# Batch 0 of a fused attention and MLP kernel: four neighbouring tokens per partition, x loaded head by head, scores by pairs of heads

## The chip, the cores and the metric

The kernel runs on one core of one Trainium2 chip. The metric is the device time of a launch in microseconds (us); a profiled execution of the same program gives the spans, busy times and waits. Engines in the profile: PE is TensorE (PEld its weight loads), DVE is VectorE, ACT is ScalarE, POOL is GpSimd, SP is SyncE; ACTq and SPq are the queues from which ScalarE and SyncE issue DMAs. A line number such as L197 is a line of the kernel before.

## The reference

A block-recurrent cross attention between tokens x and a small state, followed by an MLP with the activation `h * erf(softplus(h))` over all tokens and states. All shapes are fixed:

```python
B, H, S, Ns, D = (8, 8, 512, 32, 64)          # x: (B,H,S,D), state: (B,H,Ns,D), float32
scores  = softmax(scale * x @ state^T)        # tokens read the state
xread   = scores @ state
scores2 = softmax(scale * state @ x^T)        # the state reads the tokens
sread   = scores2 @ x
x = concat([xread, sread], axis=2)  ->  (B * (S + Ns), H * D) = (4352, 512)
h   = x @ w_in                                # (512, 2048)
g   = h * erf(softplus(h))
out = g @ w_out                               # (2048, 512)
```

Tokens of a batch are independent in everything but the sum over tokens in `sread`. So they may be kept in any order inside the kernel, as long as the rows of `out` are written back in theirs.

## The kernel before

One core works through the eight batches one after the other. A batch's tokens need x with the features on the partitions (`xT`: for pair i of heads, 64 features of head 2i on partitions 0 to 63 and 64 of head 2i+1 on partitions 64 to 127). For batches 1 to 7 this is made far ahead. Batch 0 is the start of the program, and nothing can run before it, so it has its own code, `attention0`. Meanwhile the weights, which come as float64 and are converted to float32 on ScalarE and VectorE, are loaded behind x on the SyncE queue.

Loads of batch 0. x is loaded in four quarters of 128 tokens, token 128c+p on partition p; one head's part of a token is 64 floats, 256 bytes:

```python
x_t[0] = xin.tile([P, NC, H, D], F32, name="x")
for c in range(NC):                                            # L108
    (nc.scalar, nc.sync)[c % 2].dma_start(
        out=x_t[0][:, c], in_=x[0, :, P * c:P * c + P].rearrange("h p d -> p h d"))
for e in range(2):
    nc.sync.dma_start(out=st[:, 0, D * e:D * e + D],
                      in_=state[0].rearrange("(i e) n d -> e i n d", e=2)[e])
# ... and then, on the same queue, the weights
```

Filler products keep TensorE working while it would wait:

```python
def warm(n):
    for _ in range(n):
        last = nc.tensor.matmul(out=spare[:, 0:P], lhsT=ident, rhs=ident, start=True, stop=True)
```

The score products (state against tokens, contraction over 64 features). There are eight, two (e = 0, 1) for each pair of heads i, and each fills its own 64x32 part of the array:

```python
def scored(b, xT):
    s2 = [ps_at.tile([P, S], F32, name="at") for _ in range(2)]
    for i in reversed(range(NI)):
        for e in range(2):
            r, q = slice(D * e, D * e + D), slice(Ns * i, Ns * i + Ns)
            on_pe = nc.tensor.matmul(out=s2[e][q, :], lhsT=st[r, b, q], rhs=xT[r, i, :],
                                     start=True, stop=True)     # L197
    ...
```

The opening of batch 0. TensorE transposes 128 tokens of two heads at a time; the four quarters are taken as they land. Then four copies, two on ScalarE and two on VectorE, bring the four pairs from PSUM to `xT`; the state is turned; then the scores:

```python
warm(8)                                                         # in the main program, before
...
def attention0(between):
    xt = x_t[0]
    xT = att.tile([P, NI, S], F32, name="xT")
    xp = [ps_o.tile([P, S], F32, name="o%d" % i) for i in range(3)]
    xp.append(ps_h.tile([P, S], F32, name="h"))
    for c in 1, 0, 2, 3:
        if c == 2:
            warm(3)
        for i in range(NI):
            nc.tensor.transpose(out=xp[i][:, P * c:P * c + P],  # L304
                                in_=xt[:, c, 2 * i:2 * i + 2, :], identity=ident)
    for i in range(NI):
        (nc.scalar.copy, nc.vector.tensor_copy)[i % 2](xT[:, i, :], xp[i])   # L307
    states(range(1), ps_h, "h")                                 # L182, L183
    s2 = scored(0, xT)                                          # L197
    between[0]()            # 32 fillers; the first weight conversion on ScalarE
    ...
    a = states_weights(0, s2, both)   # VectorE: 32x32 transposes (L217), max, subtract; ScalarE: exp
    ...                               # sums, normalise, transposes (L321): aT, with weights converted between
```

After that come the first projection (L714), the activation and the second projection (L550) of batch 0's first column group. The order of the instructions on TensorE, VectorE, ScalarE and SyncE is held fixed in this part as written.

The output rows of a batch are stored by quarters, 2 KB to a row:

```python
def put_x(b, h):
    rows = out[TB * b:TB * b + S].rearrange("(c p) e -> c p e", p=P)
    def go(r, ot, c=slice(0, d_model)):
        nc.sync.dma_start(out=rows[2 * h + r][:, c], in_=ot[:, c])
```

Of the kernel before, what the change touches and what calls it, by code (L numbers as in the profile page):

```python
# [8 lines left out]
F32 = mybir.dt.float32  # L9
# [7 lines left out]
def kernel(  # L17
# [17 lines left out]
    nc = tc.nc  # L35
    B, H, S, D = x.shape
    Ns = state.shape[2]
    d_model, d_ff = moe_w_in.shape
    P = 128
    NI = H // 2  # L40
    NC = S // P
# [4 lines left out]
    TB = S + Ns  # L46
# [5 lines left out]
    xin = ctx.enter_context(tc.tile_pool(name="xin", bufs=1))  # L52
# [6 lines left out]
    ps_at = ctx.enter_context(tc.tile_pool(name="ps_at", bufs=2, space=PSUM))  # L59
# [3 lines left out]
    ident = const.tile([P, P], F32, name="ident")  # L63
    make_identity(nc, ident)

    x_t = {}


    def load_x(b):
        t = xin.tile([P, NC, H, D], F32, name="x")  # L70
        for h in range(H):
            nc.sync.dma_start(out=t[:, :, h, :], in_=x[b, h].rearrange("(c p) d -> p c d", p=P))
        x_t[b] = t
# [30 lines left out]


    st = const.tile([P, B, P], F32, name="st")
    x_t[0] = xin.tile([P, NC, H, D], F32, name="x")
    for c in range(NC):  # L108
        (nc.scalar, nc.sync)[c % 2].dma_start(
            out=x_t[0][:, c], in_=x[0, :, P * c:P * c + P].rearrange("h p d -> p h d"))  # L110
    for e in range(2):
        nc.sync.dma_start(out=st[:, 0, D * e:D * e + D],
                          in_=state[0].rearrange("(i e) n d -> e i n d", e=2)[e])

    def load_st():
        for h in range(H):
            i, e = h // 2, h % 2
            nc.sync.dma_start(out=st[Ns * i:Ns * i + Ns, 1:B, D * e:D * e + D],
                              in_=state[1:B, h].rearrange("b n d -> n b d"))
# [46 lines left out]
    def warm(n):  # L166

        for _ in range(n):
            last = nc.tensor.matmul(out=spare[:, 0:P], lhsT=ident, rhs=ident, start=True,
                                    stop=True)  # L170
        return last
# [5 lines left out]
    def states(bs, pool=ps_at, name="at"):  # L177


        ps = pool.tile([P, len(bs), P], F32, name=name)  # L180
        for k, b in enumerate(bs):
            last = nc.tensor.transpose(out=ps[:, k], in_=st[:, b, :], identity=ident)  # L182
        nc.scalar.copy(st[:, bs[0]:bs[-1] + 1, :], ps)  # L183
        return last
# [2 lines left out]

    marks = []

    def scored(b, xT):  # L190


        s2 = [ps_at.tile([P, S], F32, name="at") for _ in range(2)]
        for i in reversed(range(NI)):
            for e in range(2):
                r, q = slice(D * e, D * e + D), slice(Ns * i, Ns * i + Ns)
                on_pe = nc.tensor.matmul(out=s2[e][q, :], lhsT=st[r, b, q], rhs=xT[r, i, :],  # L197
                                         start=True, stop=True)
        marks.append(on_pe)
        return s2  # L200
# [10 lines left out]
    def states_weights(b, sc, both):  # L211

        aT[b] = keep.tile([P, 2, S], F32, name="aT")
        a = both[:, 0:2].rearrange("p e (k n) -> p e k n", n=Ns)
        m1 = small.tile([P, 2, NC * NI], F32, name="m1")
        for e in range(2):
            nc.vector.transpose(out=both[:, e], in_=sc[e])  # L217
        for e in range(2):
            nc.vector.reduce_max(out=m1[:, e], in_=a[:, e], axis=AX.X)
        for e in range(2):  # L220
            nc.vector.tensor_tensor(a[:, e], a[:, e], over(m1[:, e]), op=ALU.subtract)
            nc.scalar.activation(out=a[:, e], in_=a[:, e], func=ACTF.Exp, scale=scale)
        return a

    def sums(a):
        z1 = small.tile([P, 2, NC * NI], F32, name="z1")
        for e in range(2):
            nc.vector.reduce_sum(out=z1[:, e], in_=a[:, e], axis=AX.X)
        return z1

    def normalise(a, z1):
        nc.vector.tensor_scalar(z1, z1, 1e-9, None, op0=ALU.add)
        nc.vector.reciprocal(z1, z1)
        for e in range(2):
            nc.vector.tensor_tensor(a[:, e], a[:, e], over(z1[:, e]), op=ALU.mult)

    def largest(sc):
        m2 = small.tile([P, 2], F32, name="m2")
        for e in range(2):
            nc.vector.reduce_max(out=m2[:, e:e + 1], in_=sc[:, e], axis=AX.X)  # L240
        nc.vector.tensor_scalar(m2, m2, -scale, None, op0=ALU.mult)
        return m2

    def weigh_tokens(sc, m2, a2):

        z2 = small.tile([P, 2], F32, name="z2")
        for e in range(2):
            nc.scalar.activation(out=a2[:, e], in_=sc[:, e], func=ACTF.Exp, bias=m2[:, e:e + 1],
                                 scale=scale, accum_out=z2[:, e:e + 1])
        return z2  # L250

    def inverse(z):
        nc.vector.tensor_scalar(z, z, 1e-9, None, op0=ALU.add)
        nc.vector.reciprocal(z, z)

    def turn_weights(a2):
        a2T = att.tile([P, 2, NC, P], F32, name="sc")
        for e in range(2):
            ps = ps_at.tile([P, NC, P], F32, name="at")
            for c in range(NC):  # L260
                nc.tensor.transpose(out=ps[:, c, :], in_=a2[:, e, P * c:P * c + P],
                                    identity=ident)
            nc.scalar.copy(a2T[:, e], ps)
        return a2T
# [3 lines left out]
    def read_tokens(b, a2T, z2, pool=ps_at, name="at"):  # L268


        xt = x_t.pop(b)
        sr = pool.tile([P, 2, D], F32, name=name)
# [3 lines that stand above are left out]
                    q = slice(Ns * i, Ns * i + Ns)  # L276
                    nc.tensor.matmul(out=sr[q, e, :], lhsT=a2T[:, e, c, q],  # L277
                                     rhs=xt[:, c, 2 * i + e, :],
                                     start=(c == 0), stop=(c == NC - 1))
        sn = sn_t[b] = const.tile([P, 2, D], F32, name="sn0") if b == 0 else \  # L280
            st[:, b - 1, :].rearrange("p (e d) -> p e d", e=2)
        for e in range(2):
            nc.vector.tensor_scalar(sn[:, e], sr[:, e], z2[:, e:e + 1], None, op0=ALU.mult)
# [8 lines left out]
    def attention0(between):  # L292

        xt = x_t[0]
        xT = att.tile([P, NI, S], F32, name="xT")
        xp = [ps_o.tile([P, S], F32, name="o%d" % i) for i in range(3)]
        xp.append(ps_h.tile([P, S], F32, name="h"))
        for c in 1, 0, 2, 3:  # L300
            if c == 2:
                warm(3)
            for i in range(NI):
                nc.tensor.transpose(out=xp[i][:, P * c:P * c + P],  # L304
                                    in_=xt[:, c, 2 * i:2 * i + 2, :], identity=ident)
        for i in range(NI):
            (nc.scalar.copy, nc.vector.tensor_copy)[i % 2](xT[:, i, :], xp[i])  # L307
        states(range(1), ps_h, "h")
        s2 = scored(0, xT)
        between[0]()  # L310
        both = att.tile([P, NI, S], F32, name="xT")
        sc = att.tile([P, 2, S], F32, name="sc")
        a = states_weights(0, s2, both)
        for e in range(2):
            nc.scalar.copy(sc[:, e], s2[e])
        between[1]()
        z1 = sums(a)
        between[2]()
        normalise(a, z1)
        for e in range(2):  # L320
            nc.vector.transpose(out=aT[0][:, e], in_=both[:, e])  # L321

        def rest():
            a2 = both[:, 2:4]
            m2 = largest(sc)
            yield
            z2 = weigh_tokens(sc, m2, a2)
            inverse(z2)
            yield
            a2T = turn_weights(a2)  # L330
            yield
            read_tokens(0, a2T, z2)
            yield

        return rest()
# [9 lines left out]
    def attention(b, xT=None):  # L345
# [40 lines left out]
        if b + 1 < B:  # L386
            load_x(b + 1)
# [231 lines left out]
        put(0, o1, slice(E2, d_model))  # L619

    def put_x(b, h):
        rows = out[TB * b:TB * b + S].rearrange("(c p) e -> c p e", p=P)

        def go(r, ot, c=slice(0, d_model)):
            nc.sync.dma_start(out=rows[2 * h + r][:, c], in_=ot[:, c])
        return go
# [118 lines left out]
    def amid_sums():  # L745
# [4 lines left out]
        warm(5)  # L750

    rest = attention0((after_scores, before_sums, amid_sums))
    g0 = group()

# [113 lines left out]
    xT, _ = turn_x(1)  # L868
# [7 lines left out]
    turn = attention(1, xT)  # L876
# [40 lines left out]
    at = [combine_a(1)]  # L917
# [8 lines left out]
    def pending():  # L926
        yield from seconds
        store(acc, lambda r, ot: put_x(0, r // 2)(r % 2, ot))

    for b in range(1, B + 1):  # L930
# [4 lines left out]
        for g, (first, second) in enumerate(groups):  # L935
# [5 lines left out]
            if b + 1 < B:  # L941

                late = b == 1
                if g == late:
                    side[6 if late else 6] = (lambda: behind(marks, next, turn)) if late else \
                        lambda old=turn: (next(old), behind(marks, next, turn))
                    turn = attention(b + 1)
# [64 lines left out]
```

## Time and profile before

Three runs gave a median of 732.15 us (732.14 to 732.15). The profiled execution spans 730.7 us.

| what | before |
|---|---|
| TensorE busy | 721.6 us, 99% of the span |
| VectorE, ScalarE busy | 524.0 us (72%), 395.6 us (54%) |
| first TensorE instruction | 1.35 us |
| first transpose of x on TensorE | 4.92 us |
| third quarter of x starts its transposes | 7.95 us |
| score products start | 10.30 us |
| VectorE's first transpose of the scores | 11.57 us |
| first projection, first product (L714) | 22.10 us |
| second projection, first product (L550) | 31.01 us |
| x of batch 0, issue to landing | 4.1 to 6.7 us for each 256 KB |

How to read it: in a timeline a row is a run of like instructions of one engine, with its start, the time from the first start to the last end, the number of records and, in square brackets, the idle time of the engine just before it and what ended it. A TensorE instruction can leave more than one record. Ends of TensorE records are modelled, so that start-to-start distances say more than durations. In the table of windows each row is a stretch of the span, with the busy time of each engine in it.

### The profile page before, as it was taken

The numbers are of one execution on the slowest core, as the hardware profiler recorded it, in microseconds if no ns is written. First come the engines' busy times: TensorE is split into PE (matmuls) and PEld (weight loads), VectorE is DVE, ScalarE is ACT, GpSimd is POOL, SyncE is SP. The second block draws the span as 40 slices with busy tenths as digits, with TensorE's granted clock in tenths as the row PEclk, the third lists the DMA queues.
The fourth block names the chain that finished last, engine by engine and source line by source line (L and its number), as shares of the span: only waits on it lengthen the run. The fifth ranks groups of instructions, "written<-read, shape, count | busy, mean of one in ns | idle before, by whom it ended". The sixth has DMA issues, their size and how long they took to land.

```text
span 730.7 us, 12128 instructions
## 1 busy us (share of the span) xinstructions
PE 721.6 (99%) x5016; PEld 588.0 (80%) x5016; DVE 524.0 (72%) x766; ACT 395.6 (54%) x498; POOL 0.7 (0%) x6
## 2 busy tenths in 40 slices
PE   8899999999999999999999999999999999999998
PEld 7434435889889888988989888988898899999996
DVE  4988887997798677867587669866686756674423
ACT  4898894665556444754455445544575434443340
POOL 0000000000000000000000000000000000000000
PEclk9999999999999999999999999999999999999999
DMA  7577842330153203310061104220111000000001
GB/s 234 174 216 241 224 94 58 87 59 30 19 99 67 50 1 66 80 30 30 1 144 27 33 1 94 60 44 9 38 50 30 30 1 30 1 30 1 30 1 29
DMA packets 139166, 46.40 MB, mean 64 GB/s; under 512 B 126696, under 2 KB 130536, under 8 KB 139112
## 3 DMA queue, kind: packets, MB, share of 16 engines
q1 hardware_dynamic: 136840, 44.92, 24.6%
q10 hardware_dynamic: 2272, 0.72, 0.5%
q8 instruction: 39, 0.64, 0.4%
q14 instruction: 15, 0.12, 0.1%
HBM read 33.03 MB, written 8.91 MB: 57 GB/s over the span
## 4 chain that ended last, share of the span: by engine, by line
PE 92%; DVE 2%; ACT 1%; issue 0%; ACTq 0%
PE o L600 50%; PE h L493 27%; PE o L550 7%; PE at L407 2%; PE h L407 1%; PE h L714 1%; PE at L197 1%; PE at L421 1%; PE h L277 1%; DVE s L727 0%; PE at L277 0%; DVE hs L721 0%; ACT L724 0%; DVE w_out L148 0%; ACT s L724 0%
## 5 line engine op out<-in xcount | busy, mean ns | idle before, releaser
L600 PE MATMUL o<-w_out,s 128*128 128x256 f32 x480 | 118.0, 380 | 0.0
L600 PE MATMUL o<-raw,hs 128*128 128x256 f32 x480 | 117.3, 382 | 0.0
L500 ACT ACTIVATE s<-hs 128x512 f32<-128x512 f32 x120 | 75.4, 630 | 74.3 <-DVE hs L501 74.0
L600 PE MATMUL o<-w_out,hs 128*128 128x256 f32 x480 | 114.1, 380 | 0.0
L600 PEld LDWEIGHTS o<-raw,hs 128*128 128x128 f32 x480 | 89.9, 190 | 22.6 <-issue 10.9
L501 DVE TENSOR_TENSOR hs<-hs,h 128x512 f32<-128x512 f32 x90 | 61.8, 687 | 62.6 <-PE h L493 62.4
L600 PEld LDWEIGHTS o<-w_out,hs 128*128 128x128 f32 x480 | 90.8, 190 | 16.3 <-issue 4.2
L600 PEld LDWEIGHTS o<-w_out,s 128*128 128x128 f32 x480 | 84.6, 191 | 7.9
L501 DVE TENSOR_TENSOR hs<-s,h 128x512 f32<-128x512 f32 x60 | 41.1, 685 | 67.6 <-PE h L493 67.1
L493 PEld LDWEIGHTS h<-aT,m 128*128 128x128 f32 x672 | 83.8, 192 | 4.3 <-issue 1.4
L493 PE MATMUL h<-aT,m 128*128 128x128 f32 x672 | 84.4, 275 | 0.0
L545 DVE TENSOR_TENSOR s<-s,hs 128x2048 f32<-128x2048 f32 (+1 forms) x31 | 68.8, 2218 | 20.4 <-ACT s L543 20.4
L504 ACT COPY s<-h 128x512 f32<-128x512 f32 x29 | 17.0, 585 | 107.7 <-PE h L493 107.7
L550 PE MATMUL o<-w_out,s 128*128 128x512 f32 x128 | 59.1, 600 | 0.6 <-DVE s L727 0.5
L493 PE MATMUL h<-sy,sx 128*128 128x128 f32 x448 | 59.4, 275 | 0.0
L493 PEld LDWEIGHTS h<-sy,sx 128*128 128x128 f32 x448 | 56.7, 192 | 2.1 <-issue 0.5
L543 ACT ACTIVATE s<-s 128x2048 f32<-128x2048 f32 x30 | 57.4, 1912 | 0.3
L509 ACT COPY hs<-h 128x512 f32<-128x512 f32 x29 | 17.0, 585 | 74.8 <-PE h L493 74.8
L600 PE MATMUL o<-raw,s 128*128 128x256 f32 x240 | 56.8, 379 | 0.0
L550 PEld LDWEIGHTS o<-w_out,s 128*128 128x128 f32 x128 | 23.1, 190 | 31.1 <-issue 25.8
L600 PEld LDWEIGHTS o<-raw,s 128*128 128x128 f32 x240 | 43.5, 190 | 4.7
L500 ACT ACT_TABLE_LOAD x31 | 39.8, 1283 | 0.5
(133 smaller groups left out, 915.4 us busy)
## 6 DMA issues: line engine op xcount, KB each, us to landing
raw<-in_moe_w_in_dram SPq DMA_DIRECT2D x8, 1024.0 KB, 5.7
raw<-in_moe_w_out_dram SPq DMA_DIRECT2D x8, 1024.0 KB, 4.8
xq<-in_x_dram SPq DMA_DIRECT2D x112, 64.0 KB, 2.2
x<-in_x_dram SPq DMA_DIRECT2D x56, 128.0 KB, 2.8
out_dram<-ot SPq DMA_DIRECT2D x18, 256.0 KB, 2.2
sc<-xT SPq DMA_DIRECT2D x112, 32.0 KB, 1.9
out_dram<-ot SPq DMA_DIRECT2D x28, 128.0 KB, 1.9
x<-in_x_dram ACTq DMA_DIRECT2D x2, 256.0 KB, 5.7
```

The source lines that it names most:

```text
L197: on_pe = nc.tensor.matmul(out=s2[e][q, :], lhsT=st[r, b, q], rhs=xT[r, i, :], start=True, stop=True)
L277: nc.tensor.matmul(out=sr[q, e, :], lhsT=a2T[:, e, c, q], rhs=xt[:, c, 2 * i + e, :], start=(c == 0), stop=(c == NC - 1))
L407: nc.tensor.matmul(out=ps[k][e][q, :], lhsT=st[r, b, q], rhs=w_in[r, 2 * g:2 * g + 2, i, :], start=True, stop=True)
L493: last = nc.tensor.matmul(out=bank[:, q], lhsT=lhsT, rhs=rhs, start=(first and i == 0 and k == 0), stop=(i == GF - 1 and k == len(ops) - 1 ...
L500: nc.scalar.activation(out=s[:, k], in_=hs[:, k], func=ACTF.Softplus)
L501: add = lambda o, x, y: nc.vector.tensor_tensor(o, x, y, op=ALU.add)
L504: copy(m1, p)
L509: copy(c11, p)
L543: nc.scalar.activation(out=s, in_=s, func=ACTF.Erf)
L545: nc.vector.tensor_tensor(s[:, k], s[:, k], hs[:, k], op=ALU.mult)
L550: nc.tensor.matmul(out=acc[r], lhsT=gT[:, i, P * r:P * r + P], rhs=w_out[:, GF * g + i, :], start=(g == 0 and i == 0), stop=(g == NG - 1 a ...
L600: nc.tensor.matmul(out=acc[bank][:, E2 * c:E2 * c + E2], lhsT=lhs[:, i, :], rhs=rhs[:, g, i, :], start=(first and i == 0 and c == 0), stop ...
```

## The change

Four things change, all for batch 0:

- Partition p holds the tokens 4p to 4p+3, so that one head's part of a partition is 1 KB in a row, in DRAM and on the chip.
- x is loaded head by head, the even heads on ScalarE's queue and the odd heads on SyncE's, with the state's two halves after the first head of each.
- TensorE turns x one pair of heads at a time. With heads outside and tokens inside, a pair's features no longer lie side by side, so each head is turned by itself, by a plain product with the identity into its half of the partitions. The copies to `xT` and the score products follow pair by pair, behind the turning of the next pair.
- The rows of `out` of batch 0 are stored in the new order (row 4p+c instead of 128c+p).

It is meant to bring x in larger runs and to start on the first heads while the last ones are still under way.

```diff
-    x_t[0] = xin.tile([P, NC, H, D], F32, name="x")
-    for c in range(NC):
-        (nc.scalar, nc.sync)[c % 2].dma_start(
-            out=x_t[0][:, c], in_=x[0, :, P * c:P * c + P].rearrange("h p d -> p h d"))
-    for e in range(2):
-        nc.sync.dma_start(out=st[:, 0, D * e:D * e + D],
-                          in_=state[0].rearrange("(i e) n d -> e i n d", e=2)[e])
-
+    x_t[0] = xin.tile([P, H, NC, D], F32, name="x").rearrange("p h c d -> p c h d")
+
+    def load_x0(queue, h, n):
+        queue.dma_start(out=x_t[0][:, :, h:h + n, :].rearrange("p c h d -> p h c d"),
+                        in_=x[0, h:h + n].rearrange("h (p c) d -> p h c d", c=NC))
+
+    def load_st0(queue, e):
+        queue.dma_start(out=st[:, 0, D * e:D * e + D],
+                        in_=state[0].rearrange("(i e) n d -> e i n d", e=2)[e])
+
+    for i in range(NI):
+        for e, queue in enumerate((nc.scalar, nc.sync)):
+            load_x0(queue, 2 * i + e, 1)
+            if i == 0:
+                load_st0(queue, e)
@@
-    def scored(b, xT):
-        s2 = [ps_at.tile([P, S], F32, name="at") for _ in range(2)]
-        for i in reversed(range(NI)):
+    def scored(b, xT, s2=None, pairs=tuple(reversed(range(NI)))):
+        s2 = s2 or [ps_at.tile([P, S], F32, name="at") for _ in range(2)]
+        for i in pairs:
@@
-        for c in 1, 0, 2, 3:
-            if c == 2:
-                warm(3)
-            for i in range(NI):
-                nc.tensor.transpose(out=xp[i][:, P * c:P * c + P],
-                                    in_=xt[:, c, 2 * i:2 * i + 2, :], identity=ident)
-        for i in range(NI):
+        s2 = [ps_at.tile([P, S], F32, name="at") for _ in range(2)]
+
+        def turn(i):
+            for c in range(NC):
+                for e in range(2):
+                    nc.tensor.matmul(out=xp[i][D * e:D * e + D, P * c:P * c + P],
+                                     lhsT=xt[:, c, 2 * i + e, :], rhs=ident, start=True,
+                                     stop=True)
             (nc.scalar.copy, nc.vector.tensor_copy)[i % 2](xT[:, i, :], xp[i])
+
+        turn(0)
         states(range(1), ps_h, "h")
-        s2 = scored(0, xT)
+        turn(1)
+        warm(2)
+        scored(0, xT, s2, (0,))
+        turn(2)
+        scored(0, xT, s2, (1,))
+        turn(3)
+        scored(0, xT, s2, (2,))
+        warm(3)
+        scored(0, xT, s2, (3,))
@@
-        rows = out[TB * b:TB * b + S].rearrange("(c p) e -> c p e", p=P)
+        rows = out[TB * b:TB * b + S].rearrange("(p c) e -> c p e" if b == 0 else
+                                                "(c p) e -> c p e", p=P)
```

(The new `scored` loop body is the old one.)

## The prediction

> **What bounds the kernel now.** I read three views: the table of windows by stage over the whole run (how much can a change at the start be worth, and is it given back later?), the timeline of the first 22 us (which instruction ends last before the first projection work), and the list of waits of the opening (which of those ends are waits for data).
>
> ```profile
> core 0: us, PE busy (x) PEld busy (x) DVE busy (x) ACT busy (x) POOL busy (x), PEclk, DMA share, GB/s
> 0.00:5.00 5.00, 3.65 (x17) 3.60 (x18) 0.00 (x0) 1.28 (x1) 0.70 (x6) 1.00 0.66 135
> 5.00:11.57 6.57, 5.29 (x42) 3.90 (x42) 1.29 (x2) 1.32 (x4) 0.00 (x0) 1.00 1.15 327
> 11.57:22.10 10.53, 9.26 (x90) 8.52 (x90) 10.33 (x17) 8.90 (x12) 0.00 (x0) 1.00 0.48 172
> 22.10:31.00 8.90, 8.01 (x32) 3.02 (x32) 8.74 (x11) 7.00 (x10) 0.00 (x0) 1.00 0.56 197
> 31.00:60.00 29.00, 28.70 (x94) 11.90 (x95) 24.67 (x27) 27.12 (x31) 0.00 (x0) 1.00 0.75 233
> ```
>
> From 31 us on TensorE is the bound (28.70 of 29.00 us busy, then 69.63 of 70 and 570.00 of 570 in the later rows of the same answer). Between 11.57 and 31 us VectorE is (10.33 of 10.53 and 8.74 of 8.90 us). Only the first 11.57 us, up to the end of batch 0's scores, have no such full engine, and the change lies wholly in them. What follows is in fixed order on each engine, so whatever the change wins or loses at 11.57 us should reach the end one to one: VectorE has 0.2 us of room before 31 us and TensorE 0.3 us after it.
>
> ```profile
> 1.35 3.78 PE L169 MATMUL o<-ident 128*128 128x128 f32 x16 [1.35 <-POOL ident masks.py:199]
> 4.92 0.86 PE L304 MATMUL o<-ident,x 128*128 128x128 f32 x3
> ...
> 7.95 0.55 PE L304 MATMUL o<-ident,x 128*128 128x128 f32 x3 [0.32 <-DMA x<-in_x_dram]
> ...
> 8.77 0.27 PE L304 MATMUL h<-ident,x 128*128 128x128 f32 x1
> 9.22 0.30 PE L182 MATMUL h<-ident,st 128*128 128x128 f32 x1 [0.18 <-DMA st<-in_state_dram]
> 10.30 1.09 PE L197 MATMUL at<-xT,st 64*32 64x512 f32 x16 [0.78 <-DVE xT L307]
> ```
>
> Columns: start, us, engine, line, tiles, form, count, then the idle time before it and what ended it. The reader is to see a chain with holes: the third and fourth quarters of x arrive at 7.95 us, st at 9.2 us, the copies of xT end at 10.15 us, and all eight score products (16 records) then take 1.09 us together, so that they end at 11.39 us and VectorE's transposes begin at 11.57 us. TensorE's own holes add up to about 1.5 us: 0.32 + 0.18 + 0.78, and the filler.
>
> **What the skill says.** (1) "TensorEngine Tiling (Array Packing)", Key Properties: tiles of the array work at the same time, but "Changing tiling mode (not just tile) drains the TensorE". The trace agrees on both: eight 64x32 tiles finish 16 records in 1.09 us, and the 24 records of 512 columns at 31.01 us take 10.57 us, 0.44 us each, so sixteen in a row would be 7 us. (2) The same page, Restrictions: column tiling excludes the transpose mode for FP32. That is why the changed code uses plain products. (3) "FP8 and Floating Point Precision", TensorE Precision Notes: true FP32 takes 4 passes. In the trace a plain FP32 product with the identity has two records (8 issued at 1.35 us, x16 shown), a transpose has one. (4) "DMA: Bandwidth & Descriptors", Why a DMA increments its semaphore by 16 and not by 1: the engines that a transfer uses follow from its slowest dimension; state's is 4, so it uses 4 of 16 engines. This fits st landing last of all here; no row shows the engines themselves.
>
> **The change part by part.**
> *Loads.* x of batch 0 (1 MB) goes from 4096 runs of 256 B to 1024 runs of 1 KB. In 2 to 7 us the queues moved 222 GB/s with 256 B runs; in 9 to 13 us 415 GB/s with runs of 2 KB and more. I estimate 300 to 400 GB/s for 1 KB, that is 2.7 to 3.7 us for x and st instead of about 5. The first two heads should land near 3.3 us, st near 5 instead of 9.1, the last two heads (whose issue, in the built program, waits until the first two have landed) near 6 to 7 us instead of 7.9. Weights then land no later than now, and ScalarE starts to convert them a little earlier, which frees nothing, as its exponential waits for VectorE.
>
> *Transposes.* 16 transposes of one record become 32 plain products with 64 columns of weights, 2 records each: 64 records of 128 columns, of which the two halves (e = 0, 1) sit in two column tiles and run together. At full clock one 128-column record takes 0.11 us (the 64 fillers from 11.32 us take 7.41 us); at the half speed of the opening 0.21 to 0.22 us (the 16 from 1.35 us take 3.5 us to the next start). A pair of heads is 16 records in two tiles, so 8 x 0.11 = 0.88 us, or 8 x 0.213 = 1.70 us in the slow opening, against 4 x 0.11 = 0.44 us now.
>
> *Scores.* They were 16 records in eight tiles: two rounds of 0.43 us, 1.09 us with the last one's latency. Pair by pair only two of the eight tiles (64x32, e = 0 and 1) work at a time, and each has two records of 512 columns one behind the other: 2 x 0.43 = 0.86 us for each pair, 3.4 us for four. This is the part that I take to be overlooked: the score products were already packed, and the change unpacks them.
>
> *Switches of tile form.* From 64x32 at 41.51 us (16 records of 256 columns: two rounds of 0.21 us) to 128x128 at 42.10 us is 0.59 us. Of that 0.43 are the rounds and 0.07 the stagger of eight tiles, so some 0.09 us is the switch. The new order has ten of them.
>
> *The sum on TensorE*, which has no hole left to wait in:
> - fillers end 4.95 us, as now;
> - pair 0 at the half clock: 0.1 + 1.70, to 6.8; transpose of st 0.2, to 7.0 (the clock rises near 6.9 us now: at 6.64 us the fillers become faster);
> - pair 1: 0.09 + 0.88, to 8.0; two fillers 0.09 + 4 x 0.11, to 8.5;
> - scores 0: 0.09 + 0.86, to 9.45; pair 2, 0.97, to 10.4; scores 1, to 11.4; pair 3, to 12.35; scores 2, to 13.3;
> - three fillers 0.09 + 6 x 0.11, to 14.05; scores 3, 0.95, to 15.0.
> Data are never late in this: heads 2 and 3 are needed at 7.0, heads 4 and 5 at 9.5, heads 6 and 7 at 11.4 us; copies to xT (0.6 to 0.7 us) lie beside the next pair.
> Today the last score record begins to stream about 0.59 us before its modelled end at 11.39, so its stream ends at 11.2 us, and VectorE starts 0.35 us after that. So VectorE starts at 15.35 instead of 11.57 us: +3.8 us.
>
> *Output.* Batch 0's rows leave with a stride of four rows but still 2 KB each; no cost. Later batches are untouched.
> Sum: 732.15 + 3.8, rounded down for what might overlap: 735.8 us.
>
> **The rivals.**
> (a) Data set the end, as the change supposes. For it: the waits at 7.95, 9.22 and 10.30 us. If the new products cost no more than the old, the end would be: last heads at 6.5, pair 3 0.9, copy 0.9, scores 0.95, so about 9.5 to 10 us, a gain of 1.5 to 2 us: 730.5. Against it: 64 records for 16 and four unpacked score steps; TensorE can't finish them before about 12.5 us even without any switch or filler.
> (b) Tiles of different form overlap, so that scores of one pair run beside the transposes of the next. Each such overlap is worth up to 0.9 us and there are two or three: 733.5 to 734.5. Against it: the skill's sentence on drains, and the fact that the score tile of pair 0 or 1 lies in the columns of the first half that the next pair needs.
> (c) The clock stays at half speed longer, because the array is half filled in the opening: until about 10 us this costs 1.5 us more, 737.3. No row speaks for it; the present kernel rises after 5.5 us of steady work.
> (d) The loss is absorbed by slack further on: 732 to 733. Against it: the rows of windows above.
>
> **Range and chances.** 735.8 is the sum. (b) and part of (d) give the lower end, 733.7; (c) the upper, 737.4. Rival (a) I give one in eight. A bound of 2% is 14.6 us, more than the whole stretch concerned (11.57 us), so a gain of 2% is almost excluded; a loss of 2% would need a stall that none of these parts has.
>
> **What would show it.** In the changed profile the first VectorE transpose of at should start near 15.3 us, and every later start (the first projection, now 31.01 us) be later by the same amount. Pair by pair, the 16 transposing records should take some 0.9 us and the four score records 0.9 to 1.0 us (first start to next start). The rows of TensorE between 7 and 15 us should show almost no idle time for DMA. x should land by 7 us and st by 5 to 6. If instead the wait "DMA x" or "DVE xT" stands ahead of the last score records, with VectorE starting before 11.57 us, (a) holds and my count of the products is wrong; if VectorE starts at 13 us, tiles of different form overlap; if the 128-column records still take 0.21 us at 9 us, it is (c). If VectorE starts late but 31.01 us isn't shifted, it is (d).

## The result, and the profile after

The changed kernel takes 736.81 us (median of 4 runs, 736.72 to 737.42) against 732.15 us before (4 runs, 732.14 to 732.36): 4.66 us more, a ratio of 1.0065 with a 95% interval of 1.0047 to 1.0082. The profiled execution is the slowest of the four (737.42 us); it spans 735.5 us.

Line numbers have moved: the fillers L169 are now L178, the transposes and products of x L304 are L314, the state's transpose L182 is L191, the scores L197 are L206, the copies to xT L307 are L317, VectorE's first transpose L217 is L226, the first projection L714 is L735 and the second L550 is L570.

The table of windows of the changed kernel, with the borders moved to where its stages begin:

```profile
core 0: us, PE busy (x) PEld busy (x) DVE busy (x) ACT busy (x) POOL busy (x), PEclk, DMA share, GB/s
0.00:5.00 5.00, 3.65 (x16) 3.48 (x16) 0.00 (x0) 1.08 (x1) 0.70 (x6) 1.00 0.54 156
5.00:16.49 11.49, 11.49 (x97) 6.77 (x97) 1.77 (x3) 3.73 (x6) 0.00 (x0) 1.00 0.89 301
16.49:27.00 10.51, 9.28 (x89) 8.45 (x88) 10.31 (x17) 7.14 (x10) 0.00 (x0) 1.00 0.18 49
27.00:36.00 9.00, 8.12 (x33) 3.05 (x32) 8.84 (x12) 7.08 (x10) 0.00 (x0) 1.00 0.56 192
```

The second row says what bounds the opening now. Before, TensorE was busy 5.29 of 6.57 us there; now it is busy 11.49 of 11.49 us. An opening that waited for data has become one that TensorE fills. The rows after it are those of before, some 4.5 us later: VectorE is busy 10.31 of 10.51 us and 8.84 of 9.00 us.

The timeline of the changed kernel (start, us, engine, line, tiles, form, number of records; in brackets the idle time before and what ended it):

```profile
5.06 1.98 PE L314 MATMUL o<-ident,x 128*64 128x128 f32 x16
6.97 0.48 PE L191 MATMUL h<-ident,st 128*128 128x128 f32 x1
7.38 1.12 PE L314 MATMUL o<-ident,x 128*64 128x128 f32 x16
8.43 0.71 PE L178 MATMUL o<-ident 128*128 128x128 f32 x4
9.07 1.05 PE L206 MATMUL at<-xT,st 64*32 64x512 f32 x4
10.05 1.09 PE L314 MATMUL o<-ident,x 128*64 128x128 f32 x16
11.07 1.05 PE L206 MATMUL at<-xT,st 64*32 64x512 f32 x4
12.05 1.09 PE L314 MATMUL h<-ident,x 128*64 128x128 f32 x16
13.08 1.05 PE L206 MATMUL at<-xT,st 64*32 64x512 f32 x4
14.06 0.94 PE L178 MATMUL o<-ident 128*128 128x128 f32 x6
14.92 1.05 PE L206 MATMUL at<-xT,st 64*32 64x512 f32 x4
15.90 7.41 PE L178 MATMUL o<-ident 128*128 128x128 f32 x64
16.11 1.31 DVE L226 STREAM_TRANSPOSE xT<-at 128x512 f32<-128x512 f32 x2 [2.22 <-PE at L206]
...
26.64 3.67 PE L735 MATMUL h<-aT,m 128*128 128x512 f32 x8 [0.33 <-DVE aT L341]
...
35.53 1.98 PE L570 MATMUL o<-w_out,s 128*128 128x512 f32 x4 [0.24 <-DVE s L748]
```

Two things are to be seen. No TensorE row of the opening has a bracket any more: nothing waits for DMA, for copies or for the state. And VectorE starts at 16.11 instead of 11.57 us (+4.54), the first projection at 26.64 instead of 22.10 (+4.54), the second at 35.53 instead of 31.01 (+4.52). The loss is made in the opening and carried on unchanged.

The loads are not in the way. The view of the tile x gives the time from issue to landing as minimum, median and maximum; in the changed kernel, for each 128 KB:

```profile
DMA to landing us min/median/max: 2.6/3.7/4.1
```

The last of the eight is issued at 3.6 us, so x is there by 7.7 us at the latest, and its last pair is first touched at 12.05 us.

### The profile page after: what moved, and what is told of

Same layout as the page of the kernel before. It is cut to its first block, busy times and chain, and to the rows that moved or that the text cites. A ratio compares the mean times of both kernels' runs of the same rounds, so it can differ in the third digit from the quotient of the medians.

```text
span 735.5 us, 12235 instructions
## 1 busy us (share of the span) xinstructions
PE 727.2 (99%) x5068; PEld 590.2 (80%) x5068; DVE 524.1 (71%) x766; ACT 395.6 (54%) x498; POOL 0.7 (0%) x6
## 4 chain that ended last, share of the span: by engine, by line
PE 91%; ACT 4%; DVE 4%; issue 1%; POOLq 0%; DVEq 0%; POOL 0%; ACTq 0%
PE o L620 49%; PE h L513 27%; PE o L570 5%; PE at L427 2%; PE at L206 2%; PE h L735 1%; PE h L427 1%; PE at L441 1%; PE o L178 1%; ACT L745 1%; ACT raw L155 1%; PE h L286 1%; PE o L314 1%; ACT s L745 1%; PE at L286 0%
## 5 line engine op out<-in xcount | busy, mean ns | idle before, releaser
L570 PE MATMUL o<-w_out,s 128*128 128x512 f32 x128 | 59.1, 600 | 0.6 <-DVE s L748 0.5
L570 PEld LDWEIGHTS o<-w_out,s 128*128 128x128 f32 x128 | 23.1, 190 | 31.1 <-issue 25.8
```

The source lines that it names most:

```text
L570: nc.tensor.matmul(out=acc[r], lhsT=gT[:, i, P * r:P * r + P], rhs=w_out[:, GF * g + i, :], start=(g == 0 and i == 0), stop=(g == NG - 1 a ...
```

## The experiments

Each kernel was timed beside the kernel before on the same chip, whose median was 732.34 us for the first eight and 732.30 us for the last three. "Over before" is the difference of the medians. My theory: TensorE bounds the changed opening, through unpacked scores and plain products; the rivals are the loads, and waits on data or copies.

**Scores together.** The four pairs are scored at the end in one packed group; all else is as changed.

```diff
-        scored(0, xT, s2, (0,))
         turn(2)
-        scored(0, xT, s2, (1,))
         turn(3)
-        scored(0, xT, s2, (2,))
         warm(3)
-        scored(0, xT, s2, (3,))
+        scored(0, xT, s2)
```

> Edit: the changed kernel, but all eight score products are issued together after the fourth pair has been turned, as before the change. Theory (TensorE's own work sets the end; pair by pair only two of eight tiles work, about 0.98 us a pair): three score steps and their changes of tile form fall away, some 0.9 to 1.0 us each; VectorE's first transpose starts near 13.1 instead of 16.11 us and the time falls by 3.0 us to about 733.8. Rival (the early scores fill time in which TensorE would wait for data or copies): the time stays at 736.8 or rises.

Measured: 733.96 us (733.45 to 734.52), ratio 1.0021 (1.0013 to 1.0029), 1.62 us over before instead of 4.66. Its timeline:

```profile
5.07 1.57 PE L314 MATMUL o<-ident,x 128*64 128x128 f32 x16
6.57 0.33 PE L191 MATMUL h<-ident,st 128*128 128x128 f32 x1
6.83 1.09 PE L314 MATMUL o<-ident,x 128*64 128x128 f32 x16
7.85 0.71 PE L178 MATMUL o<-ident 128*128 128x128 f32 x4
8.49 1.09 PE L314 MATMUL o<-ident,x 128*64 128x128 f32 x16
9.42 1.04 PE L314 MATMUL h<-ident,x 128*64 128x128 f32 x16
...
11.35 1.09 PE L206 MATMUL at<-xT,st 64*32 64x512 f32 x16
12.37 7.41 PE L178 MATMUL o<-ident 128*128 128x128 f32 x64
12.62 1.31 DVE L226 STREAM_TRANSPOSE xT<-at 128x512 f32<-128x512 f32 x2 [1.42 <-PE at L206]
```

The same 16 score records take 1.02 us from start to start (11.35 to 12.37) where they took four times 0.98 us. That is 2.9 us, most of the loss. The row at 8.49 is worth a look too: followed by products of its own form it takes 0.93 us, followed by the scores 1.02 us in the changed kernel (10.05 to 11.07). So the switch from these products to the scores is some 0.09 us.

**Whole transposes instead of plain products.** Scores stay pair by pair. In the new layout two neighbouring tokens of one head lie side by side, 128 numbers, and can be turned by one real transpose. Tokens of even number then stand on partitions 0 to 63, odd ones on 64 to 127, so that the state is needed on both halves and is turned twice (once with its halves exchanged), and the score tiles are chosen by parity. Each score product is cut in two by parity, so that a pair has eight records of 256 columns instead of four of 512; the columns stay, and so does the time from start to start, 0.98 us. In the cut below `xh` is the tile of x as it is stored.

```diff
-            for c in range(NC):
-                for e in range(2):
-                    nc.tensor.matmul(out=xp[i][D * e:D * e + D, P * c:P * c + P],
-                                     lhsT=xt[:, c, 2 * i + e, :], rhs=ident, ...)
+            for e in range(2):
+                for c in range(0, NC, 2):
+                    w = P * (2 * e + c // 2)
+                    nc.tensor.transpose(out=xp[i][:, w:w + P], identity=ident,
+                        in_=xh[:, 2 * i + e, c:c + 2, :].rearrange("p c d -> p (c d)"))
```

> Edit: the changed kernel, scores still pair by pair, but x is turned in transposes of one record each, two neighbouring tokens of one head at a time (the state is turned twice, the second time with its halves exchanged, so that both token parities find it on their partitions). Theory: the turning of a pair falls from 16 records in two tiles (1.0 us, 1.9 us at the start) to 4 records (0.44 us, 0.85 at the start); VectorE starts near 13.8 us and the time is about 734.5. Rival (plain products are not what costs): 736.8.

Measured: 735.59 us (735.03 to 735.71), ratio 1.0042 (1.0027 to 1.0057), 3.25 us over before. VectorE started at 14.03 us, near what I expected, but the total missed by 1 us. One cause is a side effect of the edit: parity now stands where the head stood, so the first product of the first projection needs both of VectorE's last transposes, not one. From VectorE's start to the first projection it is 11.12 us instead of 10.53; 0.2 us of that are made up by the second projection, which starts 8.68 us after the first instead of 8.89, so that 0.4 us stay. Another 0.2 us is VectorE's later start. The rest, half a microsecond, fits the reference that I took: the 16.11 us belong to an execution 0.6 us above the changed kernel's median.

**Both.** Transposes, and scores in one group; loads and fillers as in the changed kernel.

> Edit: both edits together, the scores packed and the turning in one-record transposes; loads as in the changed kernel. Theory: what is left is what the new loads are worth; the last heads land near 7.35 us and VectorE starts near 10.9 instead of 11.57 (before) or 16.11 us: about 731.5, that is 0.6 us under the kernel before. Rival (the new loads or the order by heads cost time themselves): 732.2 or more.

Measured: 732.26 us (731.42 to 732.79), ratio 0.9999 (0.9990 to 1.0007), 0.08 us under before. So plain products and unpacked scores together account for the whole 4.7 us: with both undone and the loads, the fillers and the order by pairs kept, the time is that of before. The gain is less than expected, and the trace shows the same side effect:

```profile
10.08 1.31 DVE L227 STREAM_TRANSPOSE xT<-at 128x512 f32<-128x512 f32 x2 [1.26 <-PE at L342]
...
21.20 3.67 PE L764 MATMUL h<-aT,m 128*128 128x512 f32 x8 [0.93 <-DVE aT L367]
```

VectorE is 1.49 us ahead of before (10.08 against 11.57), the first projection only 0.90 us (21.20 against 22.10); it waits 0.93 us for aT where it waited 0.33.

**No fillers.** The changed kernel without its five fillers in the opening.

```diff
         turn(1)
-        warm(2)
         scored(0, xT, s2, (0,))
@@
         scored(0, xT, s2, (2,))
-        warm(3)
         scored(0, xT, s2, (3,))
```

> Edit: the changed kernel without its two and three filler products between the pairs. Theory: TensorE has no hole there, so the fillers' 0.64 and 0.87 us lie wholly on the path: VectorE starts near 14.65 us, 735.3. Rival (they only fill waits): 736.8, unchanged; or slower, if the clock drops.

Measured: 735.32 us (734.84 to 735.60), ratio 1.0039 (1.0024 to 1.0054): 1.7 us less than the changed kernel, as the rows of the two filler groups say (0.64 and 0.87 us). They had nothing left to fill. VectorE started at 13.42 us, 1.2 us before what I expected; the profiled execution is the fastest of the four, and its timeline shows why:

```profile
5.05 1.09 PE L314 MATMUL o<-ident,x 128*64 128x128 f32 x16
6.08 0.33 PE L191 MATMUL h<-ident,st 128*128 128x128 f32 x1
6.34 1.09 PE L314 MATMUL o<-ident,x 128*64 128x128 f32 x16
```

Up to 6.34 us this kernel issues the same instructions as the changed one. There pair 0 and the state took 2.32 us (5.06 to 7.38), in the first experiment 1.76 us (5.07 to 6.83), here 1.29 us. In these three executions TensorE leaves its slow opening rate at three different moments.

**Loads by pairs.** The changed kernel with x loaded two heads at a time, a pair on each queue in turn.

```diff
-        for e, queue in enumerate((nc.scalar, nc.sync)):
-            load_x0(queue, 2 * i + e, 1)
-            if i == 0:
-                load_st0(queue, e)
+        queue = (nc.scalar, nc.sync)[i % 2]
+        load_x0(queue, 2 * i, 2)
+        if i < 2:
+            load_st0(queue, i)
```

> Edit: the changed kernel, x of batch 0 loaded in four DMAs of a pair of heads instead of eight of a head (no load waits for an earlier one to land). Theory: data are nowhere late, so VectorE's first transpose stays where TensorE puts it, 16.1 us when the clock rises near 7 us and up to 1 us earlier when it rises sooner; the DMA count is that of the kernel before, so the closing waits on DMAs should shrink by about 0.25 us: 735.7 to 736.5. Rival (the loads set the opening): VectorE starts clearly earlier, below 735.

Measured: 736.90 us (736.51 to 736.98), ratio 1.0061 (1.0048 to 1.0074), 4.56 us over before; VectorE started at 16.13 us. Loads can be changed in the new opening and nothing happens to it. The time is 0.4 us above the range that I gave: the close (from the start of VectorE's last instruction to the end) is shorter in the profile, 3.6 us against 3.9, but the median gained only 0.1 us of it. The loads are now 256 KB each, as before the change. The view of x of the kernel before, and of this one:

```profile
DMA to landing us min/median/max: 4.1/5.3/6.7
```

```profile
DMA to landing us min/median/max: 3.5/4.3/5.5
```

The median is 1 us shorter, but x isn't complete sooner. Before, all four loads are issued by 1.3 us, and the last takes 6.7 us; here the last two are issued at 2.0 and 2.4 us, and the last takes 5.5 us. In both x is complete between 7.9 and 8.0 us. Sooner are the first loads, issued at 0.7 us in both: 3.5 and 3.8 us instead of 4.1 and 4.8 us.

**All together.** Transposes, packed scores, loads by pairs, no fillers, the state turned late, the last pair copied on ScalarE, and the last transposes of VectorE taken by heads, which is meant to remove the side effect. The cut shows what differs from "both", without the loads, which are those above, and the copy.

```diff
         turn(0)
-        swapped()
         turn(1)
-        warm(2)
         turn(2)
+        swapped()
         turn(3)
-        warm(3)
@@
-            nc.vector.transpose(out=aT[0][:, e], in_=both[:, e])
+            w = slice(2 * P * e, 2 * P * e + 2 * P)
+            nc.vector.transpose(out=aT[0][:, :, w], in_=both[:, 0:2, w])
```

> Edit: everything at once: pair loads, one-record transposes, packed scores, no fillers between, the last pair copied on ScalarE, and the last VectorE transposes by heads, so that the first projection's first product waits for one of them. Theory: the third and fourth pairs are turned as they land (6 to 7 us), VectorE starts at 9.4 to 10 us instead of 11.57 and the whole is 1.6 to 2.1 us faster than the kernel before: 730.2 to 730.8. Rival (some other wait of the opening, st or the weights, takes over): 731.5 or more.

Measured: 732.38 us (731.51 to 735.93, 14 runs), ratio 1.0008 (0.9998 to 1.0018). A miss: the time lies where the rival had it, but the wait that took over was for x itself, not for st or the weights. TensorE was through with its first two pairs early and waited:

```profile
4.72 1.09 PE L317 MATMUL o<-ident,x 128*128 128x128 f32 x8
...
7.49 0.66 PE L317 MATMUL o<-ident,x 128*128 128x128 f32 x4 [1.67 <-DMA x<-in_x_dram]
...
10.66 1.31 DVE L227 STREAM_TRANSPOSE xT<-at 128x512 f32<-128x512 f32 x2 [1.60 <-ACT w_in L154]
```

With cheap products the landing of the third pair, seen at 7.49 us, is the next bound. (The bracket of VectorE's row names ScalarE's conversion of w_in, which ended at the same moment. But VectorE starts 0.2 us after the start of TensorE's next row, at 10.46 us, just as in the changed kernel, so that the scores fit as its releaser too.) VectorE starts at 10.66 us, 0.9 us ahead of before in this execution, but its runs scatter over 4.4 us and their median is that of before.

**Short runs.** The changed kernel's tokens and loads (token 4p+c, head by head), but on the chip a token's heads lie side by side as before, so that a run is 256 bytes there; in DRAM it is still 1 KB. A pair's features then lie side by side: transposes and state as before, turned pair by pair, scores packed.

```diff
-    x_t[0] = xin.tile([P, H, NC, D], F32, name="x").rearrange("p h c d -> p c h d")
+    x_t[0] = xin.tile([P, NC, H, D], F32, name="x")
@@
+            for c in range(NC):
+                nc.tensor.transpose(out=xp[i][:, P * c:P * c + P],
+                                    in_=xt[:, c, 2 * i:2 * i + 2, :], identity=ident)
```

> Edit: heads loaded one by one in the changed kernel's order, but into the layout of before (256 B runs), in which a pair's features lie side by side: sixteen one-record transposes, packed scores, fillers as in the changed kernel. It differs from the run with both edits mainly in the length of the runs. Theory: at about 220 GB/s the last heads land near 8.5 to 9 us instead of 7.4, VectorE starts near 11.5 us and the time is about 732.3. Rival (1 KB runs bring nothing): the last heads land by 7.5 us, 731.5 or less.

Measured: 732.78 us (732.48 to 736.27, 15 runs), ratio 1.0013 (1.0006 to 1.0021), 0.44 us over before and 0.5 us more than expected. Its profiled execution, the slowest of its runs, waited 2.52 us for the last pair:

```profile
10.92 1.12 PE L313 MATMUL h<-ident,x 128*128 128x128 f32 x4 [2.52 <-DMA x<-in_x_dram]
```

From issue to landing the median of its eight loads is 3.8 us, and 3.7 in the changed kernel; only the longest differs, 6.9 against 4.1 us. The same plan with runs of 1 KB ("both", above) lay 0.52 us lower over before, in spite of its wait for aT, and "heads last" below, without that wait, 0.99 us. So the longer runs do seem to help an opening that goes head by head, by 0.5 to 1.0 us in the medians; those two kernels also differ from this one in how the scores and the state are laid out.

**Four more transfers.** All kernels above that load x in eight parts closed later than before. To see whether it is the number of transfers, the kernel before was given four more, far from the opening: four of its loads of the later batches' states are cut in two. Nothing else differs.

```diff
-            nc.sync.dma_start(out=st[Ns * i:Ns * i + Ns, 1:B, D * e:D * e + D],
-                              in_=state[1:B, h].rearrange("b n d -> n b d"))
+            for bs in ((slice(1, 4), slice(4, B)) if h < 4 else (slice(1, B),)):
+                nc.sync.dma_start(out=st[Ns * i:Ns * i + Ns, bs, D * e:D * e + D],
+                                  in_=state[bs, h].rearrange("b n d -> n b d"))
```

> Edit: the kernel before, with four of the eight later state loads split in two, that is four DMAs more, far from any path, as many as the change adds. Reason: in the changed kernel's profile the time from the last VectorE row to the end is 3.89 us, before 3.64. Theory: the semaphores of the last stores move on by four, SyncE's closing waits run through them in a fixed order, and a store that lands late is now waited for first instead of last: VectorE's first transpose stays at 11.57 us and the end is 0.2 to 0.4 us later, 732.4 to 732.6. Rival (the longer close has to do with the opening or is chance): 732.2 to 732.3 as before.

Measured: 733.04 us (732.91 to 734.50, 21 runs), ratio 1.0014 (1.0008 to 1.0021), 0.70 us over before, more than expected. The opening isn't later (VectorE at 11.38 us) and the last VectorE instruction starts at 726.89 us against 727.09 us, but the span ends at 731.2 us against 730.7. The waits of SyncE in the last microseconds (line waited for, us in total, times, longest), of the kernel before:

```profile
SPq L1007 <- DMA out_dram<-ot: 1.1, 3, 0.5
SPq L1007 <- PEq L1007: 0.6, 2, 0.4
```

of the kernel with four more transfers:

```profile
SPq L1008 <- DMA out_dram<-ot: 1.4, 1, 1.4
SPq L1008 <- PEq L1008: 0.6, 2, 0.4
```

and of the changed kernel, which has four more transfers as well:

```profile
SPq L1028 <- DMA out_dram<-ot: 1.2, 1, 1.2
SPq L1028 <- PEq L1028: 0.3, 2, 0.2
```

At the end SyncE waits for the output's transfers. Before, three waits of at most 0.5 us follow each other; with four more transfers there is a single wait of 1.2 to 1.4 us. All eight profiled kernels with four more transfers than before show the single wait and end 3.9 to 4.3 us after the last VectorE instruction's start; the four with as many as before, itself among them, show three waits and end 3.6 us after it, and one with eight more (below) three waits and 3.8 us.

**Heads last, fillers kept.** The version with both undone, and the side effect removed as in "all together".

```diff
-            nc.vector.transpose(out=aT[0][:, e], in_=both[:, e])
+            w = slice(2 * P * e, 2 * P * e + 2 * P)
+            nc.vector.transpose(out=aT[0][:, :, w], in_=both[:, 0:2, w])
```

> Edit: the run with both edits (loads by heads, one-record transposes, packed scores, fillers), and in addition VectorE's last transposes taken by heads instead of by token parity. There, VectorE's first transpose was 1.49 us earlier than before but the first projection only 0.90 us, as its first product waited for two of these transposes instead of one. Theory: the projection gains 0.5 to 0.6 us, 731.7 to 731.8 in the median (732.26 without). Rival (something else holds the projection): 732.2 to 732.3.

Measured: 731.75 us (731.18 to 732.50, 13 runs), ratio 0.9994 (0.9985 to 1.0002). The median is as expected, the best of the study and 0.55 us under before, with an interval that just takes in 1. The profiled execution is the slowest of the 13, and its last pair came late:

```profile
8.32 0.66 PE L317 MATMUL h<-ident,x 128*128 128x128 f32 x4 [0.74 <-DMA x<-in_x_dram]
...
10.97 1.31 DVE L227 STREAM_TRANSPOSE xT<-at 128x512 f32<-128x512 f32 x2 [1.26 <-PE at L342]
...
21.63 3.67 PE L765 MATMUL h<-aT,m 128*128 128x512 f32 x8 [0.46 <-DVE aT L368]
```

From VectorE's start to the first projection it is 10.66 us instead of 11.12, so the edit does what it was meant to. At the second projection 0.2 us of that are left (19.58 us after VectorE's start instead of 19.80), less than half of the 0.47 us by which the median lies under that of "both", each over before; that the number came out as expected is in part luck.

**The same, with the four state loads cut as well**, so that there are eight more transfers than before, and SyncE's closing waits should fall as before.

> Edit: the last run, with four of the eight later state loads split in two, so that the whole number of DMAs is eight more than before and the last stores get the semaphores that they have in the kernel before. Theory (the close depends on which semaphores the last stores have): another 0.3 to 0.7 us, 731.0 to 731.5, faster than the kernel before. Rival (the closing 0.7 us of the lanes run came from the splitting itself): slower than the last run, by some 0.3 us or more.

Measured: 731.79 us (730.91 to 732.57, 13 runs), ratio 0.9993 (0.9985 to 1.0001). A miss, though the rival, a loss, didn't come either: the closing waits did fall as before (three, the longest 0.4 us), and the profiled execution closed 0.2 us faster than that of the last run, but the median gained nothing.

**All together, with nine fillers.** To steady the version that scattered, five fillers after the second pair and four after the last. The cut shows what differs from "all together".

```diff
         turn(1)
+        warm(5)
         turn(2)
         swapped()
         turn(3)
+        warm(4)
         scored0(range(NI))
```

> Edit: the kernel with everything at once (pair loads), with five filler products after the second pair and four after the fourth. Reason: without fillers its times ran from 731.5 to 735.9 us, and the long ones had a lower granted TensorE clock (0.994 to 0.998). Theory: TensorE waited 1.7 us for the third pair just where the clock is about to rise, and in some runs it rose some us later or fell back; with fillers the spread falls to under 1.5 us, the clock to 0.999 and more, and the median to 731.0 to 731.6. Rival (the spread has another cause): as wide as before.

Measured: 732.62 us (731.89 to 733.33, 13 runs), ratio 1.0004 (0.9995 to 1.0012). The scatter fell from 4.4 to 1.4 us, and no run was granted a clock under 0.999, where five of the 14 without fillers had 0.994 to 0.998. But the median didn't fall: the wait for the third pair remained (1.49 us, until 8.35 us).

## Why the prediction was right

**Only the opening counts, one to one.** Right: +4.54, +4.54 and +4.52 us at three places, +4.66 us in the time. Rival (d), absorption, is out. What I left out is the close: 3.9 us from the last VectorE instruction to the end instead of 3.6. The experiment with four more transfers, which leaves the opening alone, has the longer close too.

**TensorE, not data, sets the changed opening.** Right, by the row without a hole and by the loads by pairs, which moved nothing. Rival (a), data set the end, is out for the changed kernel; with cheap products TensorE did wait for x in some of the profiled executions (1.67 us with all together, 0.74 us with heads last, not at all with both).

**Unpacking the scores is the main cost.** Right: undoing it alone takes off 3.0 us of 4.66 (from 4.66 to 1.62 over before).

**Plain products cost the rest.** Right: undoing them as well takes off 1.7 us, although that edit brought its own wait of 0.6 us, of which 0.4 us stayed.

**Forms don't overlap.** Right: the steps of 1.02 and 0.98 us follow one another in full, so rival (b) is out. The records that the prediction puts beside the skill's two sentences show only the first, that tiles work side by side; for the drain it had its estimate of 0.09 us alone. The Trainium skill, "TensorEngine Tiling (Array Packing)", Key Properties, has the drain without a figure; here the switch measures some 0.09 us from the products to the scores. **The slow rate ends early**: right, pair 1 runs at 1.05 us from 7.38 us on, so rival (c) is out.

**The sizes.** The time came out 1.0 us above the prediction, inside the range. In the profiled execution VectorE started 0.76 us later than the sum said (16.11 against 15.35), and the terms can be read off start to start:

| term of the sum | predicted | measured |
|---|---|---|
| pair 0 at the slow rate | up to 6.8 us | up to 6.97 us |
| the state's transpose | 0.2 us | 0.41 us |
| two fillers, three fillers | 0.53, 0.75 us | 0.64, 0.87 us |
| a later pair with its switch | 0.97 us | 1.02 us |
| a score step with its switch | 0.95 us | 0.98 us |

Half of the 0.76 us lies in the first two rows, where I let the clock rise "near 6.9 us" and counted the transpose at the fast rate. In that execution the slow rate lasted through it; in others it ended up to 1 us sooner. No row waits for a load or a copy. The remaining 0.3 us is the close. Two side sums of the prediction are off, and nothing rests on them: the three holes that it counts make 1.28 us, and 2.3 with the filler (0.98 us), not 1.5; and its steps without switch or filler end at 12.9 us, not 12.5.

**The gain that was meant.** x does arrive sooner, but by less than I estimated. In the changed kernel the first head lands 2.6 us after its issue at 0.7 us, where the first quarter of x took 4.1 us; the last head takes 3.8 us from 3.6 us on and is there at 7.4 us, not at 6 to 7; before, the last to land was the third quarter, at 7.9 us (the fourth, at 7.2 us, didn't land with it, as the prediction has it). The last head also varies: with heads last its pair was waited for until 8.32 us. The state came as predicted: with the same loads, in "both", VectorE waited for its second half until 5.71 us; before, TensorE waited for it until 9.22 us.

In the profile of the kernel with both undone VectorE started 1.49 us earlier than before, with 0.90 us left at the first projection, 1.15 us at the last VectorE instruction and 0.8 us at the end of the span (729.9 against 730.7 us), as the close is 0.4 us longer. But that execution took 731.76 us, and the median of the 12 runs, 732.26 us, is only 0.08 us under before. What the slower runs lost isn't shown, as only one was traced. The varying end of the slow rate and the varying landing of the last head are candidates. The close is a weak one: four more transfers cost the kernel before 0.70 us, but setting the closing waits as before again gained nothing in the median.

## What to carry to other kernels

Before work is cut into pieces so that it can start earlier, look at how many tiles of the array it fills at once: eight packed 64x32 products took 1.02 us, the same eight by twos 3.9 us, and x complete half a microsecond sooner could not pay for that. Ask of a new layout in memory what the next engine has to do with it: here it cost twice the TensorE time for the turning (0.93 us for a pair of heads instead of 0.44), until a transpose was found that takes the layout as it lies. And compare when data are there, not how long each load took: with loads by pairs the longest took 5.5 us instead of 6.7, and x was complete no sooner. Fillers, last, are for holes; once TensorE is the bound they are simply added (1.5 us here).

## What the runs showed of the hardware

- The moment at which TensorE leaves its slow rate isn't fixed. With the same instructions on TensorE up to then, in three kernels, pair 0 and the state took 1.29, 1.76 or 2.32 us. The Trainium skill says so in "TensorE: Matmul & The Clock Gate", Part 1: The HAM clock gate: the window over which the clock gate watches TensorE's activity is free-running, so it doesn't begin with the kernel. The prediction took one execution's moment for a constant. The kernel before seems not to feel it: 46 of its runs on one chip lay within 0.50 us and 33 on another within 0.70 us, while the 14 runs with scores together spread over 1.07 us and the 12 with both over 1.37 us. That its wait for data, at 7.95 us, hides the moment is my reading.
- The close of these kernels went with the number of transfers issued long before. In all 13 profiles SyncE's closing waits fall as that number has it, with 0.2 to 0.7 us between kernels that differ in little else. In the medians it isn't clear: 0.70 us in one pair of kernels, 0.1 us and nothing in two others. That the order of the waits is the reason is my reading; only the number of transfers, and the size of those that were cut, was varied.
